# Tiles that DMA fills on 256-byte boundaries, in chunked attention followed by a routed expert layer

## The chip, the core and the metric

The kernel runs on one core of one Trainium2 chip. The metric is the device time of one execution in microseconds (us). Before the change three runs took 704.83, 706.77 and 709.05 us; the median is 706.77 us. A separate execution was recorded by the hardware profiler. Engines are named as in the profile: PE is TensorE, with PEld for its weight loads; DVE is VectorE; ACT is ScalarE; POOL is GpSimd; SP is SyncE. L12 means line 12 of the kernel before.

## What is computed

Attention inside chunks of 64 tokens, then a layer in which a router gives each token to one of eight experts. Everything is fp32.

```python
# q, k, v: (B=8, H=8, S=576, Dh=64); chunks of 64 tokens, each on its own
scores = q_c @ k_c.T / sqrt(64);  attn = softmax(scores);  x = attn @ v_c
x = x.transpose(0, 2, 1, 3).reshape(4608, 512)            # N tokens, D
logits = (x / |x|) @ (expert_emb / |expert_emb|).T / tau   # 8 experts
e = argmax(logits);  gate = softmax(logits)[e]
out = gate * (relu(x @ w1[e]) @ w2[e])                     # w1: 512x1024, w2: 1024x512
```

## The kernel before

**Attention.** The 4608 tokens are taken as 36 tiles of 128 tokens (two chunks each). For each tile the kernel loads q and k (`load_qk`, L560: 128 partitions, eight pieces of 64 floats, that is 256 bytes, per partition), turns them with TensorE (`turn_qk`, L583), multiplies q by k (`scores`, L599), subtracts the maximum and takes the exponential, turns the result (`turn_a`, L625), multiplies it by v (`values`, L639) and divides, which leaves 128 token rows in a slot of `xr`. The stages of successive tiles are interleaved in a loop that is written out by hand, and every engine works through its own list in program order. The loads of q and k go four tiles ahead, into four buffers each; from the fifth tile on they are issued by GpSimd, while SyncE issues v (`load_v`, L572), one batch of 576 tokens at a time into one of two tiles `v_sb`. Before the loads of the fifth tile GpSimd also writes all constants (`constants`, L497 to L533), among them zeros in the tails of `xr` and in `blank`.

**The token store.** A router (`turn_x`, `logits`, `pick`, `place`) finds the expert of each token and its place in a store in device memory, `spots`, one region per expert. Every token is one record: 512 floats of x and a tail of 16 floats with its eight logits, its token number and the sum of its squares. `xr` has eight such records per partition, one for each of the last eight tiles. One put per tile (`put`, L779), an indirect DMA that GpSimd issues, scatters 128 records into the store. `xr`'s slot is written again eight tiles later; L656 is the first write into it. At the start SyncE clears the first rows of two experts' regions from `blank` (`clear_first`, L540 and L544), and four last puts write `blank` into the places left empty.

**The expert layer.** Blocks of 128 rows (two groups of 64, one for each half of the experts) are loaded from the store by SyncE (`load_rows`, L145, in pieces of 128 floats, and L151 for the tail), three blocks ahead in `xin`. TensorE multiplies them by w1 (L245 for the first blocks; L334, in a form with seven products of half size that works on sums of weight blocks) and by w2 (`result`, L405); GpSimd scatters the rows to the output (L420). Weights for the first blocks come with `load_first` (L120). Later ones come with `load_when` (L169), which SyncE issues only where a block's expert differs from that in the buffer, into `w2_sb` or `next_w1`.

**Where tiles lie.** Tiles are given addresses inside a partition one after another in the order in which they are allocated, pool after pool: `keep` (weights, block numbers, `xin`, `spot`), `blk`, then for the attention `qk`, `work` and `one` (v, `xr`, constants). When these three are closed, pool `late` takes their place for w2's second buffers, `next_w1`, `sums` and the work tiles of the products. The first user of such a tile waits for the last users of what lay there before.

Of the kernel before, what the change touches and what calls it, by code (L numbers as in the profile page):

```python
# [9 lines left out]
FP32 = mybir.dt.float32  # L10
# [8 lines left out]
P = 128  # L19
# [6 lines left out]
def kernel(  # L26
# [11 lines left out]
    nc = tc.nc  # L38
    B, H, S, Dh = q.shape
    E, D = moe_expert_emb.shape  # L40
    F = moe_w1.shape[2]
    N = B * S
    NPAIR = H // 2
# [3 lines left out]
    NCB = S // CH  # L47
    G = P // 2
# [11 lines left out]
    XBUF = 3  # L60
# [9 lines left out]

    MW = 16
    W = D + MW
    TOK, SQ = E, E + 1
    R = N + G * NE
    SPARE = E * R
    spots = nc.dram_tensor("spots", (SPARE + G, W), FP32, kind="Internal").ap()

    keep = ctx.enter_context(tc.tile_pool(name="keep", bufs=1))  # L80
    ctx.enter_context(tc.manual_schedule())

    w1_sb = [keep.tile([P, KD, F], FP32, name=f"w1_{s}") for s in range(2)]
    w2_sb = [[keep.tile([P, KF, D], FP32, name=f"w2_{s}0")] for s in range(2)]

    w1_rows = moe_w1.rearrange("e (p c) f -> p e (c f)", c=KD)
    w2_rows = moe_w2.rearrange("e (p c) d -> p e (c d)", c=KF)
# [15 lines left out]
    n_steps = keep.tile([1, 1], I32, name="n_steps")  # L105
    n_odd = keep.tile([1, 1], I32, name="n_odd")
    second = keep.tile([P, 1], FP32, name="second")
    xin_sb = [keep.tile([P, D], FP32, name=f"xin{i}") for i in range(XBUF)]
    SPOTS = 8
    spot = keep.tile([P, SPOTS, MW], FP32, name="spot")  # L110
    bp = ctx.enter_context(tc.tile_pool(name="blk", bufs=2))

    def whole(w):
# [12 lines left out]
    xin, mo = {}, {}  # L126
# [10 lines left out]
    def load_rows(j, rows):  # L137

        xin[j] = xin_sb[j % XBUF]
        ins = []  # L140
        for s in range(2):
            for b in range(G // Q if s < len(rows) else 0):
                c = s * (G // Q) + b
                ins.append(
                    nc.sync.dma_start(  # L145
                        out=xin[j][:, c * P : c * P + P],
                        in_=rows[s][Q * b : Q * b + Q, 0:D].rearrange("i (r d) -> r i d", d=P),
                    )
                )
            ins.append(  # L150
                nc.sync.dma_start(out=spot[G * s : G * s + G, j % SPOTS], in_=rows[s % len(rows)][:, D:W])  # L151
            )
        return ins

    def load_x(j):
        rows = []
        for s in range(2 if j != LEAST else 1):
            row = number(src_row[of_step(s, j)], SPARE, ENG.SP)
            rows.append(spots[ds(row, G), :])
        load_rows(j, rows)  # L160

    def first_rows(s, j, n):
        r0 = (0, E - 1)[s] * R + G * j
        return spots[r0 : r0 + G * n, :]
# [44 lines left out]
    def gate_parts(j):  # L209
        lg = spot[:, j % SPOTS, 0:E]  # L210
        rn = bp.tile([P, 1], FP32, tag="rn", name="rn", bufs=4)
        lmax = bp.tile([P, 1], FP32, tag="lmax", name="lmax", bufs=4)
        sh = bp.tile([P, E], FP32, tag="sh", name="sh", bufs=4)
        last = "_last" if j == LEAST - 1 else ""
        gate = bp.tile([P, 1], FP32, tag="gate" + last, name="gate", bufs=5)
        nc.scalar.activation(rn, spot[:, j % SPOTS, SQ : SQ + 1], AF.Sqrt)  # L216
        yield
        nc.vector.tensor_reduce(lmax, lg, axis=AX.X, op=ALU.max)
        nc.vector.tensor_scalar(rn, rn, 1e-6, None, ALU.add)  # L219
        nc.vector.reciprocal(rn, rn)  # L220
        nc.vector.tensor_scalar(sh, lg, lmax, rn, ALU.subtract, ALU.mult)
        yield
        nc.scalar.activation(sh, sh, AF.Exp, accum_out=gate)  # L223
        yield
        nc.vector.tensor_scalar(gate, gate, 1e-9, None, ALU.add)
        nc.vector.reciprocal(gate, gate)
        gate_of[j] = gate
# [169 lines left out]
    def result(j, ps_y):  # L397
# [15 lines left out]
        nc.scalar.activation(y[:, 0:w], ps[:, 0:w], AF.Copy, scale=gate_of.pop(j))  # L413
        to, at, bound = out, spot[:, j % SPOTS, TOK : TOK + 1].bitcast(I32), N - 1
        if one_group:
# [18 lines left out]
    RB = 4  # L434
    sizes = [RB] * (NT // RB)
    batch_of = [(b, i) for b, n in enumerate(sizes) for i in range(n)]
    VW = 72
    with (
        tc.tile_pool(name="qk", bufs=4) as qk_p,
        tc.tile_pool(name="work", bufs=2) as wk,  # L440
# [4 lines left out]
        tc.tile_pool(name="ps_l", bufs=1, space=PSUM) as ps_l,  # L445
    ):

        ident = one.tile([P, P], FP32, name="ident")
        make_identity(nc, ident)
        rt_ps = ps_l.tile([P, 4, RB, E], FP32, name="rt_ps")  # L450
# [4 lines left out]
        enT = one.tile([P, KD, E], FP32, name="enT")  # L455


        v_sb = [one.tile([P, NPAIR, NCB, VW], FP32, name=f"v{i}") for i in range(2)]
        onesb = one.tile([P, P], BF16, name="onesb")
        sltb = one.tile([P, P], BF16, name="sltb")  # L460

        NX = 2 * RB
        xr = one.tile([P, NX, W], FP32, name="xr")
        blank = one.tile([P, W], FP32, name="blank")
        io_i = one.tile([P, NST], I32, name="io_i")
        io = one.tile([P, NST], FP32, name="io")
        back = one.tile([P, NST], FP32, name="back")
# [28 lines left out]
        def constants():  # L496
# [3 lines left out]
            nc.gpsimd.memset(onesb, 1.0)  # L500
            nc.gpsimd.memset(xr[:, :, D:W], 0.0)
            nc.gpsimd.memset(blank, 0.0)
# [34 lines left out]
        def clear_first():  # L537

            for s in range(2):
                nc.sync.dma_start(  # L540
                    out=first_rows(s, 0, NE).rearrange("(j p) w -> p j w", p=G),
                    in_=blank[0:G].unsqueeze(1).to_broadcast([G, NE, W]),
                )
# [86 lines left out]
        def values(t):  # L630
# [3 lines left out]
            for i in range(NPAIR):  # L634
# [13 lines left out]
            nc.vector.reciprocal(rs, rs)  # L648
            x = xr[:, t % NX, 0:D]
            nc.vector.tensor_tensor(  # L650
# [5 lines left out]
            nc.gpsimd.iota(  # L656
                xr[:, t % NX, D + TOK : D + TOK + 1].bitcast(I32),
                pattern=[[0, 1]],
# [5 lines left out]
        def turn_x(t):  # L664
            d = st[t]
            ps = ps_t.tile([P, KD, P], FP32, tag="tr", name="tr")
            for c in range(KD):
# [5 lines left out]
            nc.scalar.activation(  # L673
                junk, d["x"], AF.Square, accum_out=xr[:, t % NX, D + SQ : D + SQ + 1]
            )
# [14 lines left out]
        def copy_logits(b):  # L690
            n, t = sizes[b], sum(sizes[:b])
            copied[b] = xr[:, t % NX : t % NX + n, D : D + E]
            nc.vector.tensor_copy(copied[b], rt_ps[:, b % 2, 0:n])
# [17 lines left out]
        def place(b):  # L711
# [33 lines left out]
            if t + n < NT:  # L745
                with nc.allow_low_precision("whole numbers up to 36 + 128"):
                    if n == 1:
                        nc.vector.tensor_tensor(before, before, eqb[:, t], ALU.add)
                    else:
# [5 lines left out]
                        )  # L755
            to_put.extend((dest[:, i : i + 1], xr[:, (t + i) % NX]) for i in range(n))

# [15 lines left out]
        def load_early(j):  # L773
            early_ins.extend(load_rows(j, [first_rows(s, j, 1) for s in range(2)]))
# [289 lines left out]
        behind()  # L1064

    late_p = ctx.enter_context(tc.tile_pool(name="late", bufs=1, reuse_waits="tile"))
    for s in range(2):
        w2_sb[s].append(late_p.tile([P, KF, D], FP32, name=f"w2_{s}1"))

# [7 lines left out]
    with (  # L1077
# [18 lines left out]
        for j in range(LEAST - 1):  # L1096
            n = j + 2
# [104 lines left out]
```

## Time and profile before

| | us |
|---|---|
| median of three runs (lowest, highest) | 706.77 (704.83, 709.05) |
| the profiled execution's own time | 710.12 |
| its span, from first to last instruction | 708.3 |
| PE busy in the span | 651.9 (92%) |
| DVE busy | 426.4 (60%) |
| ACT busy | 441.9 (62%) |
| POOL busy | 160.3 (23%) |
| mean granted TensorE clock | 0.961 |
| moved by DMA | 111.65 MB in 92,670 packets, 50,316 of them under 512 bytes |

The profile is of one execution, and sums over it are compared with its own time. A group's line gives the source line, the engine, the operation, the tiles written and read, then busy time and idle time ahead with what ended it. The granted clock is the share of full speed that TensorE was allowed. The DMA share is the busy time of the core's 16 DMA engines, averaged; [...]it can pass 1. Beside the page, the trace records every DMA packet: its queue, its start, how long it took and its size.

### The profile page before, as it was taken

What the parts mean: (1) busy time and instruction counts of PE and PEld (TensorE: products, weight loads), DVE (VectorE), ACT (ScalarE), POOL (GpSimd) and SP (SyncE); (2) the same over time, 40 slices, a digit from 0 to 9 for tenths busy, and PEclk for the clock granted to TensorE, in tenths of its full rate; (3) what the DMA queues carried; (4) which work ended last, traced back from release to release, by engine and by line L of the source; (5) the groups of instructions that cost most, each with busy time, mean ns of one, the idle gap of its engine ahead of it and who ended that gap; (6) DMA issues with size and microseconds to landing.
All of it is one profiled execution on the core that took longest, in us unless ns stands there. A gap on an engine that the chain in (4) does not pass through costs nothing. (4 is left out here: it accounts for less than half of the span.)

```text
span 708.3 us, 24825 instructions
## 1 busy us (share of the span) xinstructions
PE 651.9 (92%) x9735; PEld 384.7 (54%) x9735; DVE 426.4 (60%) x1139; ACT 441.9 (62%) x767; POOL 160.3 (23%) x241
## 2 busy tenths in 40 slices
PE   3699898998999897999999999999999999999991
PEld 2489797998754343666643444444444443444430
DVE  2478786586649853554766565776665567565520
ACT  3266565464522574767777877877777767877640
POOL 7747676473322110101000101000000100100101
PEclk9799999698999998999999999999999999999996
DMA  9989999798971771111477511486741114411110
GB/s 192 212 187 226 234 240 234 179 230 210 341 276 55 288 281 38 45 46 33 139 298 273 174 43 37 153 315 241 270 171 47 49 40 158 166 41 32 48 33 29
DMA packets 92670, 111.65 MB, mean 158 GB/s; under 512 B 50316, under 2 KB 70540, under 8 KB 92536
## 3 DMA queue, kind: packets, MB, share of 16 engines
q1 hardware_dynamic: 80552, 72.21, 34.4%
q0 software_dynamic: 11952, 37.67, 19.4%
q8 instruction: 81, 1.33, 0.8%
q14 instruction: 53, 0.43, 0.2%
q10 hardware_dynamic: 32, 0.02, 0.0%
HBM read 334.71 MB, written 21.60 MB: 503 GB/s over the span
## 5 line engine op out<-in xcount | busy, mean ns | idle before, releaser
L405 PE MATMUL y_ps<-w,hT 128*32 128x512 f32 (+1 forms) x2368 | 274.5, 590 | 4.1 <-DMA w<-in_moe_w_dram 4.1
L353 ACT ACTIVATE h<-C 64x256 f32<-64x256 f32 x264 | 178.4, 676 | 95.9 <-DVE C L366 70.8
L405 PEld LDWEIGHTS y_ps<-w,hT 128*32 128x32 f32 x2368 | 95.6, 111 | 153.2 <-issue 122.8
L420 POOL DMA_INDIRECT out_dram<-y,spot x36 | 35.0, 971 | 438.8 <-ACT C L369 208.7
L366 DVE TENSOR_TENSOR C<-C,h 128x256 f32<-128x256 f32 x231 | 96.1, 417 | 46.6 <-DVEq L291 39.7
L334 PE MATMUL h<-w,S 128*32 128x256 f32 x1056 | 98.0, 379 | 2.0 <-DVE w L283 2.0
L334 PE MATMUL h<-sums,xbT 128*32 128x256 f32 x1056 | 97.4, 379 | 0.0
L334 PE MATMUL h<-w,xbT 128*32 128x256 f32 x1056 | 79.3, 380 | 6.6 <-ACTq L291 5.4
L360 DVE STREAM_TRANSPOSE hT<-h 128x512 f32<-128x512 f32 x66 | 46.8, 708 | 45.3 <-ACT h L353 45.2
L334 PEld LDWEIGHTS h<-w,xbT 128*32 128x32 f32 x1056 | 41.3, 110 | 42.5 <-ACTq L291 13.7
L334 PEld LDWEIGHTS h<-w,S 128*32 128x32 f32 x1056 | 49.6, 110 | 23.8 <-DVE w L283 1.5
L670 ACT COPY xT<-tr 128x512 f32<-128x512 f32 x36 | 21.1, 587 | 65.4 <-PE tr L668 65.4
L334 PEld LDWEIGHTS h<-sums,xbT 128*32 128x32 f32 x1056 | 49.6, 110 | 20.6
L219 DVE TENSOR_SCALAR rn<-rn 128x1 f32<-128x1 f32 x37 | 5.7, 153 | 73.3 <-ACT rn L216 73.3
L334 PE MATMUL h<-sums,S 128*32 128x256 f32 x528 | 48.6, 379 | 0.0
L195 DVE STREAM_TRANSPOSE xbT<-xin 128x256 f32<-128x256 f32 x73 | 46.8, 679 | 0.5 <-DVE hT L360 0.5
L779 POOL DMA_INDIRECT spots<-xr,dest x36 | 37.1, 1031 | 43.3 <-ACT aT L627 12.3
L216 ACT ACT_TABLE_LOAD x34 | 43.6, 1283 | 0.9 <-issue 0.3
L223 ACT ACT_TABLE_LOAD x34 | 43.6, 1283 | 0.6
L413 ACT ACTIVATE y<-y_ps,gate 128x512 f32<-128x512 f32 (+1 forms) x37 | 25.3, 683 | 29.8 <-issue 16.3
L588 DVE COPY qxT<-tr 128x512 f32<-128x512 f32 x36 | 24.8, 689 | 24.8 <-PE tr L583 23.5
L607 DVE TENSOR_REDUCE mx<-sc 128x8 f32<-128x512 f32 x36 | 24.9, 692 | 22.6 <-PE sc L599 22.5
(195 smaller groups left out, 879.3 us busy)
## 6 DMA issues: line engine op xcount, KB each, us to landing
w<-in_moe_w_dram SPq DMA_DIRECT2D x74, 2048.0 KB
next_w<-in_moe_w_dram SPq DMA_DIRECT2D x67, 2048.0 KB
xin<-spots SPq DMA_DIRECT2D x158, 64.0 KB
qx<-in_q_dram POOLq DMA_DIRECT2D x32, 256.0 KB, 7.5
v<-in_v_dram SPq DMA_DIRECT2D x56, 144.0 KB
kx<-in_k_dram POOLq DMA_DIRECT2D x28, 256.0 KB, 7.6
spot<-spots SPq DMA_DIRECT2D x80, 4.0 KB
spots<-blank SPq DMA_DIRECT2D x2, 528.0 KB
```

The source lines that it names most:

```text
L195: nc.vector.transpose(xT[:, :, cols].rearrange("p c (b i) -> p b c i", i=Q), t[:, s * (D // 2) : (s + 1) * (D // 2)].rearrange("p (b i c) ...
L216: nc.scalar.activation(rn, spot[:, j % SPOTS, SQ : SQ + 1], AF.Sqrt)
L223: nc.scalar.activation(sh, sh, AF.Exp, accum_out=gate)
L334: nc.tensor.matmul(ps[t0 : t0 + Q], lhsT=a[:, c, s], rhs=w[:, r], start=c == 0, stop=c == KD // 2 - 1,)
L353: nc.scalar.activation(h[b][G * v : G * v + G, s].rearrange("p (k i) -> p k i", i=Q), x[G * s : G * s + G].rearrange("p (i k) -> p k i", i=Q),
L360: nc.vector.transpose(hT.rearrange("p k (s b i) -> p b s k i", b=2, i=Q)[:, b], h[b].rearrange("p s (k i) -> p s k i", i=Q),)
L366: nc.vector.tensor_tensor(out, a, b, op)
L405: nc.tensor.matmul(ps[Q * r : Q * r + Q, 0:w], lhsT=d["hT"][:, c, Q * t0 : Q * t0 + Q], rhs=w2_sb[s][buf_of(j)][:, c, d0 : d0 + w], start= ...
L413: nc.scalar.activation(y[:, 0:w], ps[:, 0:w], AF.Copy, scale=gate_of.pop(j))
L420: ins = nc.gpsimd.indirect_dma_start(out=to, out_offset=bass.IndirectOffsetOnAxis(ap=at, axis=0), in_=y[:, 0:w], in_offset=None, bounds_ch ...
L607: nc.vector.tensor_reduce(mx, sc, axis=AX.X, op=ALU.max)
L779: ins = nc.gpsimd.indirect_dma_start(out=spots, out_offset=bass.IndirectOffsetOnAxis(ap=at, axis=0), in_=m, in_offset=None, bounds_check=S ...
```

## The change

Tiles that a DMA fills are allocated together, behind small pad tiles that bring their first byte to a multiple of 256 in the partition. There are four pads, `pad_keep`, `pad_one`, `pad_qk` and `pad_late`; each is filled once by GpSimd. `xin` and `spot` move up to stand behind the weights in pool `keep`; v, `xr` and `blank` move to the front of pool `one`. A row of v, of which 65 floats are used, now takes 128 floats (512 bytes) where it took 72 (288 bytes). A token record takes 576 floats (2304 bytes) where it took 528 (2112 bytes), in `xr`, in `blank` and in the store; the 48 new floats are zeros that nothing reads. The loads of the tail still take 16 floats.

```diff
     MW = 16
-    W = D + MW
+    W = D + 64
+    RW = D + MW
...
+    def pad(pool, n, name):
+
+        if n:
+            nc.gpsimd.memset(pool.tile([P, n], FP32, tag=name, name=name, bufs=1), 0.0)
+
+    pad(keep, 32, "pad_keep")
     w1_sb = [keep.tile([P, KD, F], FP32, name=f"w1_{s}") for s in range(2)]
     w2_sb = [[keep.tile([P, KF, D], FP32, name=f"w2_{s}0")] for s in range(2)]
+    xin_sb = [keep.tile([P, D], FP32, name=f"xin{i}") for i in range(XBUF)]
+    SPOTS = 8
+    spot = keep.tile([P, SPOTS, MW], FP32, name="spot")
...
-                nc.sync.dma_start(out=spot[G * s : G * s + G, j % SPOTS], in_=rows[s % len(rows)][:, D:W])
+                nc.sync.dma_start(out=spot[G * s : G * s + G, j % SPOTS], in_=rows[s % len(rows)][:, D:RW])
...
-    VW = 72
+    VW = 2 * Dh
...
+        pad(one, 40, "pad_one")
+        v_sb = [one.tile([P, NPAIR, NCB, VW], FP32, name=f"v{i}") for i in range(2)]
+        NX = 2 * RB
+        xr = one.tile([P, NX, W], FP32, name="xr")
+        blank = one.tile([P, W], FP32, name="blank")
+        pad(qk_p, 40, "pad_qk")
         ident = one.tile([P, P], FP32, name="ident")
...
-        v_sb = [one.tile([P, NPAIR, NCB, VW], FP32, name=f"v{i}") for i in range(2)]
...
-        NX = 2 * RB
-        xr = one.tile([P, NX, W], FP32, name="xr")
-        blank = one.tile([P, W], FP32, name="blank")
...
     late_p = ctx.enter_context(tc.tile_pool(name="late", bufs=1, reuse_waits="tile"))
+    pad(late_p, 40, "pad_late")
```

More of the change, by code (lines that the diff above doesn't have):

```diff
@@ L107 @@
     second = keep.tile([P, 1], FP32, name="second")
-    xin_sb = [keep.tile([P, D], FP32, name=f"xin{i}") for i in range(XBUF)]
-    SPOTS = 8
-    spot = keep.tile([P, SPOTS, MW], FP32, name="spot")
     bp = ctx.enter_context(tc.tile_pool(name="blk", bufs=2))
```

## The prediction

> **What bounds the kernel now.** I read the table of stages first (busy time of each engine, granted TensorE clock, DMA share, GB/s; the second number on a line is the stretch's length):
>
> ```profile
> core 0: us, PE busy (x) PEld busy (x) DVE busy (x) ACT busy (x) POOL busy (x), PEclk, DMA share, GB/s
> 0.00:35.00 35.00, 16.89 (x232) 13.48 (x236) 10.91 (x23) 10.53 (x17) 27.01 (x70) 0.80 1.08 202
> 35.00:123.70 88.70, 82.60 (x1761) 75.34 (x1754) 66.10 (x160) 53.84 (x120) 56.44 (x78) 1.00 1.07 224
> 123.70:137.40 13.70, 13.29 (x155) 12.13 (x154) 7.31 (x21) 5.79 (x12) 4.88 (x7) 0.50 0.60 160
> ...
> 277.00:700.00 423.00, 410.21 (x5520) 200.22 (x5512) 245.01 (x650) 301.97 (x473) 32.06 (x33) 1.00 0.35 121
> ```
>
> Three stages. In the first 35 us TensorE works half the time, at a clock of 0.80, while the DMA engines are full (1.08): transfers bound this stage. From 35 to 205 us they stay nearly full, but TensorE is busy 82.60 of 88.70 us, so TensorE bounds it. From 277 us on it is busy 97%, and DMA runs at 0.35. Next the chain of waits, TensorE alone: the bracket is the idle time ahead of a line and what ended it.
>
> ```profile
> 3.98 1.09 PE L583 MATMUL tr<-ident,kx 128*128 128x128 f32 x4 [3.98 <-DMA kx<-in_k_dram]
> 7.19 1.12 PE L583 MATMUL tr<-ident,qx 128*128 128x128 f32 x4 [2.13 <-DMA qx<-in_q_dram]
> 17.35 1.08 PE L583 MATMUL tr<-ident,qx 128*128 128x128 f32 x4 [5.15 <-DMA qx<-in_q_dram]
> 28.73 1.09 PE L583 MATMUL tr<-ident,kx 128*128 128x128 f32 x4 [5.20 <-DMA kx<-in_k_dram]
> 31.45 1.09 PE L583 MATMUL tr<-ident,qx 128*128 128x128 f32 x4 [1.63 <-DMA qx<-in_q_dram]
> ...
> 124.11 0.69 PE L599 MATMUL sc<-kxT,qxT 64*64 64x64 f32 x11 [2.33 <-issue]
> ...
> 272.33 9.68 PE L405 MATMUL y_ps<-w,hT 128*32 128x512 f32 x62 [4.14 <-DMA w<-in_moe_w_dram]
> ```
>
> After 31.45 us TensorE waits for no q, k or v of any size: a tile of 128 tokens takes 4.1 to 4.3 us (scores begin at 42.73, 46.82, 50.91, 55.00), and GpSimd, which issues the loads, idles for a free q or k buffer instead. So faster transfers are worth something in the first 31 us, little after. The last line is a late issue, not a slow transfer: SyncE issued this conditional load at 272.13, after issuing row loads from 266.21 on, and no weight packet moved between 262 and 272.
>
> **The change, part by part.** By the addresses in the built programs, the q and k tiles start 224 bytes past a multiple of 256 before and on one after; the weight tiles go from 128 past to 0, xin and spot from 224 to 0, v from 32 and 160 past with rows 288 apart to 0 with rows 512 apart. Every engine has the same instructions in the same order, except for four small fills that GpSimd gains.
>
> *What a 256-byte boundary is worth to a packet.* The record of DMA packets can tell, because v already holds both kinds: with rows of 288 bytes, one in nine begins on a multiple of 256. In v's load near 134.5 us, which has the engines to itself, one engine's run of packets (ns taken / ns since the one before) reads
>
> ```
> 15/- 15/15 18/12 18/14 18/14 18/14 18/14 18/14 18/14 18/12 18/14 18/14 18/12 18/14 18/12 18/13 18/14 18/13 18/14 18/14 ...
> ```
>
> and goes on at 18/14 to the end of its 42 packets, one in nine of them aligned; 15 ns stand near the head of a run, for q/k tiles (never aligned) too. So: 0 ns for an aligned destination. At the source end the rows of the token store, 2112 bytes apart, begin on a boundary in one of four; of the 20,224 packets of 512 bytes that read them, 15,709 took 27 ns and 422 took 25. Again no two groups.
>
> The Trainium skill says otherwise ("DMA: Bandwidth & Descriptors", section "How a descriptor splits into AXI transactions"): a transaction must start at a multiple of 256, so a piece that starts 224 bytes past one is fetched as a whole 256 bytes for its last 32, and then 224: 15 beats of 32 bytes for 8. It describes reads. If engine time followed beats at the writing end, the start's serial legs would shrink to 8/15. These legs are qx 1.50 to 7.19, qx 11.07 to 17.35, and kx with qx from 21.79 to 31.45 (GpSimd's issue to TensorE's start): 5.7 + 6.3 + 9.7 = 21.7 us, so an estimate of 10.1 us by the rule and 0 by the row. I take the row. What it cannot tell is crowded engines: in the first 31.5 us a 4096-byte packet of GpSimd's loads (16 pieces of 256 bytes) took 329 ns in the mean, against 16 x 14.2 = 227 ns at v's undisturbed pace. If alignment won all of that, (329 - 227)/329 = 31% of 21.7 = 6.7 us. Bounds 0 and -6.7; value 0, the only measured case.
>
> *More bytes.* A token record grows from 2112 to 2304 bytes, +192. The 36 puts (L779): 128 x 192 = 24.6 KB each, 0.11 us of the engines at 224 GB/s. They lie beside TensorE-bound work, and GpSimd, with 0.9 + 0.9 us of load issues, 0.15 of L656 and 1.05 of a put, has 1.1 us of every 4.1 us tile free; without that cover 36 x 0.11 = 4.0 us. What is late next, if a put is late, is the reuse of its slot in xr, where GpSimd's L656 already waits 18.8 us in all; behind it in that queue are the next tiles' q and k, which are used four tiles (16.4 us) after their issue and land in 7. So 0. The clearing of the first rows (L540, L544) grows by 0.11 MB, 0.5 us of the engines at 202 GB/s, beside the start's q/k loads: bounds 0 and 0.5, value 0.1, since its packets run from 16.9 to 22.1, and the kx that TensorE waits for at 28.73 is only issued at 21.79.
>
> *GpSimd's queue at the start.* This row prices the fills (start, length):
>
> ```profile
> 13.73 0.20 POOL L501 MEMSET xr<- 128x128 f32 x1
> 13.88 0.54 POOL L502 MEMSET blank<- 128x528 f32 x1
> 14.47 0.10 POOL L503 MEMSET blank<- 128x1 int32 x1
> 14.51 0.10 POOL L504 MEMSET ones<- 128x8 f32 x1
> ...
> 21.79 1.50 POOL L560 DMA_DIRECT2D kx<-in_k_dram  x2 [0.22 <-issue]
> ```
>
> Three fills of 32 or 40 elements now stand ahead of ident and of every q load: small fills follow one another in 0.04 us, so 0.12 us (0.30 if each held the queue for its whole 0.10). The fill of xr grows from 8 x 16 to 8 x 64 elements: (0.54 - 0.20)/400 = 0.85 ns an element, 384 x 0.85 = +0.33; blank gains 48 elements, +0.04. Behind them, in order, wait all the constants and then kx and qx of the fifth tile, issued at 21.79, and TensorE is idle for these at 28.73 with nothing to cover it. So +0.12 + 0.33 + 0.04 = +0.49 us on the path. The fourth fill, pad_late, stands after the last put and ahead of the first output scatter, shares its place with pad_qk alone, and GpSimd is 10% busy there: 0.
>
> *Waits that move with the addresses.* next_w1_1 no longer lies over xr, so its first load loses three waits; C now lies over xr and blank, so its first use at 238.74 (L369) gains waits for the puts. The last of these was issued at 217.7 and landed 2.4 us later, 18 us ahead: 0. Behind that copy ScalarE holds a tile's gates, and TensorE's next products would be late if it were not so. The first sums_1 subtraction (233.17) drops the same finished waits: 0. Conditional weight loads at 4096 bytes took 159 ns from 128 past a boundary, and the output's packets, of which y is aligned before, 159 too (1739 of 2302): 0; the late issue at 272.13 stays.
>
> *Sum.* 0 + 0.1 + 0.49 = +0.6 us. On the profiled execution: span 708.3 + 0.6 = 708.9, with 1.8 us around it (710.12 - 708.3) 710.7. That execution lay 3.35 us above the median of 706.77; the same +0.6 on the median gives 707.4.
>
> **Rivals.** *Alignment pays where the engines are crowded.* For it: DMA share 1.08 and 329 ns where 227 would do. Against: two queues that take turns on each engine explain a longer packet as well. Worth half to all of 6.7 us, 707.4 - 3.4 = 704.0 to 707.4 - 6.7 = 700.7, and emptier engines could also remove a gap at "issue" (the 2.33 us at 124.11, with 13.7 us at half clock behind it: 2.3 + 6.8 = 9.1), which makes 698 or less. I put it at 702.
>
> *The clock falls once more (slower).* Place: any TensorE gap between 35 and 277 us. The stretch 123.70:137.40 ran at 0.50 after a gap of only 2.33 us; others followed 166.85 (a gap of 1.84) and 272.33. The record of the granted clock has half-clock stretches of 6.8 and 13.7 us there, so the price is 3.4 us for each 6.8. The Trainium skill ("TensorE: Matmul & The Clock Gate", section "Part 1: The HAM clock gate (the "warmup" mystery)") has the clock fall after an idle window of about 3.4 us, and the window run free of the kernel. By that rule gaps of 2 us cost nothing and mine would change no clock; by the row a gap of 2 us that falls badly costs 3.4, and a start 0.6 us later moves every gap against the window. Without any new gap: 707.4 + 3.4 = 710.8; it decides from one more such stretch per run. Against: before has the same lottery, and a median averages it.
>
> *The rule holds in full:* 707.4 - 10.1 = 697.3. The 18/14 row speaks against it.
>
> **How the numbers follow.** About 0.5% (3.5 us; the three runs spread from 704.83 to 709.05) is what a measurement of this kernel can tell from no change. No effect but the +0.6: 0.50, with its own range 704 to 710. Crowded engines gain: 0.24, and the full rule 0.03, nearly all below 703.2. Slower clock: 0.23, nearly all above 710.3. Hence faster 0.26, same 0.52, slower 0.22. Cutting a tenth from each side: 699 to 712.
>
> **What would show each step.** Right: v's uncrowded packets still 18 ns at a pace of 14; TensorE's waits near 17.35 and 28.73 within 0.6 us of before, GpSimd's kx issue at about 22.3; a fill of xr at 0.5 us; scores still 4.1 us apart; weight packets at 159 ns; weight-stage TensorE busy 97%. Wrong: packets of q and k clearly below 329 ns in the start and TensorE in its steady pace by 28 us (the first rival); more or longer stretches of half clock (the second); a GpSimd wait at L656 that now reaches TensorE as a wait for kx.

## The result and the profile after

Four runs of the changed kernel took 686.30 to 690.14 us, median 688.75; four runs of the kernel before, beside them, took 704.83 to 709.05, median 707.65. The ratio is 0.9734 with a 95% interval of 0.9691 to 0.9777: about 19 us faster, where the prediction had 707.4 and a range of 699 to 712. The profiled execution of the changed kernel took 686.30 us, with a span of 684.5; that of the kernel before took 710.12, with a span of 708.3. So the two traces differ by 23.8 us, more than the medians do. Executions now and then run some per cent slower as a whole; the ratios leave them out, and the one profile of such an execution (of the kernel with longer records alone, span 718.0) isn't read.

Line numbers have moved by 10 in the attention stage (L583 is now L593, L716 is L726) and by 8 in the expert layer (L405 is L413). The stages of the changed kernel, in the columns shown before:

```profile
core 0: us, PE busy (x) PEld busy (x) DVE busy (x) ACT busy (x) POOL busy (x), PEclk, DMA share, GB/s
0.00:35.00 35.00, 22.02 (x301) 18.02 (x302) 12.94 (x27) 13.00 (x22) 29.04 (x75) 0.85 0.95 241
35.00:123.70 88.70, 88.65 (x1916) 81.42 (x1917) 73.36 (x181) 57.82 (x130) 60.88 (x86) 1.00 0.87 242
123.70:137.40 13.70, 13.66 (x281) 12.43 (x280) 11.63 (x33) 8.99 (x21) 9.99 (x14) 1.00 0.98 281
...
277.00:684.00 407.00, 386.93 (x5204) 175.69 (x5194) 233.95 (x624) 288.42 (x451) 30.01 (x31) 0.99 0.35 123
```

In the first 35 us TensorE is busy 22.02 us instead of 16.89. From 35 to 123.7 us the DMA engines are busy 0.87 instead of 1.07 while they move more per second (242 instead of 224 GB/s), and TensorE has no idle time left: 88.65 of 88.70 us, where it had 82.60. The 13.7 us after that, at half clock before, run at full clock. In the expert stage the DMA share is 0.35 as before and TensorE is busy 95% (97% before). (A share above 1 needs no second queue: v's undisturbed packets take 18 ns each and follow one another every 14, so that they overlap on their own queue. The share compares kernels; it doesn't say by itself when the engines are full.)

TensorE's own lines with an idle time ahead, from 13 us to the first late load of weights:

```profile
13.35 1.09 PE L593 MATMUL tr<-ident,qx 128*128 128x128 f32 x4 [1.10 <-DMA qx<-in_q_dram]
25.68 1.09 PE L593 MATMUL tr<-ident,kx 128*128 128x128 f32 x4 [5.56 <-DMA kx<-in_k_dram]
27.60 1.09 PE L593 MATMUL tr<-ident,qx 128*128 128x128 f32 x4 [0.84 <-DMA qx<-in_q_dram]
148.92 0.34 PE L649 MATMUL pv<-v,aT 64*64 64x65 f32 x5 [0.92 <-issue]
167.37 0.18 PE L726 MATMUL rt_ps<-eqb_all,sltb 128*128 128x32 bf16 x1 [1.12 <-DVE eqb_all L717]
185.30 0.18 PE L726 MATMUL rt_ps<-eqb_all,sltb 128*128 128x32 bf16 x1 [0.76 <-DVE eqb_all L717]
...
217.91 0.62 PE L342 MATMUL h<-w,S 128*32 128x256 f32 x4 [0.96 <-DVE w L291]
219.58 1.10 PE L342 MATMUL h<-w,S 128*32 128x256 f32 x10 [1.04 <-DVE w L291]
...
251.14 7.81 PE L413 MATMUL y_ps<-w,hT 128*32 128x512 f32 x62 [2.13 <-DVE C L374]
```

And those of the kernel before, of which the prediction showed only the first part and one gap:

```profile
41.24 0.33 PE L583 MATMUL tr<-ident,kx 128*128 128x128 f32 x1 [0.81 <-issue]
77.03 0.33 PE L599 MATMUL sc<-kxT,qxT 64*64 64x64 f32 x3 [0.31 <-issue]
84.49 0.21 PE L639 MATMUL pv<-v,aT 64*64 64x65 f32 x1 [1.83 <-issue]
115.33 0.63 PE L583 MATMUL tr<-ident,kx 128*128 128x128 f32 x4 [1.17 <-DVE xr L650]
124.11 0.69 PE L599 MATMUL sc<-kxT,qxT 64*64 64x64 f32 x11 [2.33 <-issue]
166.85 0.34 PE L639 MATMUL pv<-v,aT 64*64 64x65 f32 x5 [1.84 <-issue]
188.30 0.18 PE L716 MATMUL rt_ps<-eqb_all,sltb 128*128 128x32 bf16 x1 [1.12 <-DVE eqb_all L707]
206.14 0.18 PE L716 MATMUL rt_ps<-eqb_all,sltb 128*128 128x32 bf16 x1 [0.77 <-DVE eqb_all L707]
```

The last line of that list, the last rank product (the product of `eqb_all` and `sltb` with which the router's last batch ends), is a mark that both kernels have: 206.14 and 185.30 us. So 20.84 of the 23.8 us are won ahead of it. They split into four terms. A stretch at half clock in which TensorE is never idle costs half its length (from 123.70 to 137.40 us the kernel before did 155 products at half clock, the changed one 281 at full), so half the time at half clock is counted, as an estimate.

| up to the last rank product, us | before | after | difference |
|---|---|---|---|
| end of the last start wait (for qx) | 31.45 | 27.60 | -3.85 |
| gaps at "issue" after it | 7.12 | 0.92 | -6.20 |
| other gaps after it | 3.06 | 1.88 | -1.18 |
| half of the time at half clock after it (27.4 and 8.1 us) | 13.71 | 4.05 | -9.66 |
| the rest: TensorE at work | 150.80 | 150.85 | +0.05 |

That the rest is equal to 0.05 us says that the four terms hold the whole difference of these two executions (over all the runs below the rest varies by 3 us). Behind the mark 502.2 us have become 499.2: the wait for the late issue at 272.33, 4.14 us with 6.8 us at half clock around its end, is one of 2.13 at 251.14 with none (SyncE issued the load at 250.93); 3.4 us at half clock lie at 220.0, behind the gaps of 0.96 and 1.04.

The packets themselves, from the record of each one, in ns. A "packed" packet is one of GpSimd's loads of q and k that carries 16 pieces of 256 bytes; "lone" is the median of those packed packets with no packet of v beside them; the other values are means where nothing else is said:

| packets | before | after |
|---|---|---|
| q and k by GpSimd, 16 pieces of 256 bytes, first 31.5 us | 329.5 | 212.4 |
| the same, lone | 268 | 194 |
| v, one piece of 256 bytes, first 31.5 us | 25.2 | 18.8 |
| v with no packed packet near | 18.8 | 18.2 |
| weights, 4096 bytes in one piece (median) | 159 | 159 |
| instructions, 16 KB, up to 205 us | 1199 | 1074 |

The page's sums per queue say the same, before and then after (packets, MB, share of 16 engines; q0 is GpSimd's queue):

```profile
q1 hardware_dynamic: 80552, 72.21, 34.4%
q0 software_dynamic: 11952, 37.67, 19.4%
```

```profile
q1 hardware_dynamic: 80552, 72.32, 33.2%
q0 software_dynamic: 11952, 38.56, 17.0%
```

As many packets and 0.9 MB more on q0, in a share of a span that is itself shorter.

### The profile page after: what moved, and what is told of

It is laid out like the page before. It is cut to its first block, busy times and chain, and to the rows that moved or that the text cites. A ratio compares the mean times of both kernels' runs of the same rounds, so it can differ in the third digit from the quotient of the medians.

```text
span 684.5 us, 24832 instructions
## 1 busy us (share of the span) xinstructions
PE 643.0 (94%) x9735; PEld 363.4 (53%) x9735; DVE 423.5 (62%) x1139; ACT 441.5 (65%) x767; POOL 160.5 (23%) x245
## 5 line engine op out<-in xcount | busy, mean ns | idle before, releaser
L413 PE MATMUL y_ps<-w,hT 128*32 128x512 f32 (+1 forms) x2368 | 274.4, 587 | 2.3 <-DVE C L374 2.1
L413 PEld LDWEIGHTS y_ps<-w,hT 128*32 128x32 f32 x2368 | 87.5, 110 | 159.6 <-issue 145.6
L342 PE MATMUL h<-w,S 128*32 128x256 f32 x1056 | 101.1, 380 | 2.0 <-DVE w L291 2.0
L342 PE MATMUL h<-sums,xbT 128*32 128x256 f32 x1056 | 101.1, 383 | 0.0
L342 PE MATMUL h<-w,xbT 128*32 128x256 f32 x1056 | 80.7, 380 | 6.4 <-ACTq L299 5.2
L342 PEld LDWEIGHTS h<-w,S 128*32 128x32 f32 x1056 | 48.0, 110 | 25.2 <-DVE w L291 1.5
L342 PEld LDWEIGHTS h<-sums,xbT 128*32 128x32 f32 x1056 | 48.4, 111 | 22.5 <-issue 0.8
L203 DVE STREAM_TRANSPOSE xbT<-xin 128x256 f32<-128x256 f32 x73 | 44.2, 644 | 0.5 <-DVE hT L368 0.5
L421 ACT ACTIVATE y<-y_ps,gate 128x512 f32<-128x512 f32 (+1 forms) x37 | 25.2, 682 | 29.0 <-issue 12.8
L690 PEld LDWEIGHTS rt_ps<-enT,xT 128*128 128x128 f32 x288 | 35.0, 192 | 1.1 <-issue 0.8
L570 POOL DMA_DIRECT2D kx<-in_k_dram x36 | 31.6, 881 | 16.0 <-PE tr L593 15.2
```

The costliest lines, as they stand in the source:

```text
L203: nc.vector.transpose(xT[:, :, cols].rearrange("p c (b i) -> p b c i", i=Q), t[:, s * (D // 2) : (s + 1) * (D // 2)].rearrange("p (b i c) ...
L342: nc.tensor.matmul(ps[t0 : t0 + Q], lhsT=a[:, c, s], rhs=w[:, r], start=c == 0, stop=c == KD // 2 - 1,)
L413: nc.tensor.matmul(ps[Q * r : Q * r + Q, 0:w], lhsT=d["hT"][:, c, Q * t0 : Q * t0 + Q], rhs=w2_sb[s][buf_of(j)][:, c, d0 : d0 + w], start= ...
L570: eng.dma_start(out=x[done : done + n], in_=src[b, :, s : s + n, :].rearrange("h p d -> p h d"),)
L690: nc.tensor.matmul(rt_ps[:, batch_of[t][0] % 2, batch_of[t][1]], lhsT=d["xT"][:, c], rhs=enT[:, c], start=(c == 0), stop=(c == KD - 1),)
```

## The experiments

### Which part of the change pays

Four kernels each do one part alone, or undo one. q and k alone on boundaries:

```diff
 # kernel before
+        pad(qk_p, 8, "pad_qk")
         ident = one.tile([P, P], FP32, name="ident")
```

> The kernel before with the q and k tiles alone moved from 224 past a multiple of 256 to 0 (a pad of 8 floats ahead of them); rows of v stay 288 bytes apart, records 2112. Theory Q (a piece of 256 bytes that straddles a boundary costs GpSimd's packed q/k packets extra, and the crowd then slows v): nearly all of the gain, 690 to 695 us, GpSimd's packets in the first 31.5 us down from 329 to about 215 ns in the mean, v beside them from 25 to about 19 ns. Theory V (the rows of v): 704 to 708 us and unchanged q/k packets. Theory R (records of 2304 bytes): 707 us.

v alone, rows of 512 bytes that begin on boundaries:

```diff
 # kernel before
-    VW = 72
+    VW = 2 * Dh
...
+        pad(one, 56, "pad_one")
         v_sb = [one.tile([P, NPAIR, NCB, VW], FP32, name=f"v{i}") for i in range(2)]
```

> The kernel before with v alone changed: rows 512 bytes apart, first row on a boundary; q and k stay 224 past one, records 2112 bytes. Theory Q: 703 to 708 us, q/k packets still above 270 ns. Theory V: 690 to 695 us, and both v and q/k packets short, because the crossing writes of v held the engines. Theory R: 707 us.

Token records of 2304 bytes alone:

```diff
 # kernel before
-    W = D + MW
+    W = D + 64
+    RW = D + MW
...
+        pad(one, 56, "pad_one")
         xr = one.tile([P, NX, W], FP32, name="xr")
```

> The kernel before with the token records alone changed: 2304 bytes apart in xr, in blank and in the store, xr and blank on a boundary. Theories Q and V: 707 to 709 us (36 longer puts and a fill that is 0.33 us longer). Theory R: 690 to 700 us, with shorter puts and fewer waits of GpSimd at the first write into xr.

The changed kernel with q and k back at 224 bytes past a boundary:

```diff
 # kernel after
-        pad(one, 40, "pad_one")
+        pad(one, 48, "pad_one")
...
-        pad(qk_p, 40, "pad_qk")
+        pad(qk_p, 96, "pad_qk")
```

> The changed kernel with q and k alone put back to 224 past a boundary; v, records and weights stay on boundaries. Theory Q: the gain goes, 703 to 708 us, q/k packets near 300 ns again. Theory V: 689 to 692 us. Half of each: 697 to 700 us.

Measured, as ratios to the kernel before beside them on the same chip (the ratios are those on record, not quotients of the medians): q and k alone 0.9780 (0.9729 to 0.9832), 695.55 us; v alone 0.9829 (0.9768 to 0.9890), 698.30; records alone 0.9993 (0.9938 to 1.0049); all but q and k 0.9791 (0.9731 to 0.9850), 698.16. So records are worth nothing that shows (within 4 us), q with k some 15 us, v some 12, both together 19: less than the sum. That v pays at all is the surprise, for its undisturbed packets take 18 ns with or without a boundary. With v alone moved, v's packets in the start take 22.5 ns and the lone packed ones still 268; with q and k alone moved, 21.2 and 195. The mean of all packed packets in the start, 329.5 before and 212.4 after, is 265.5 with q and k alone moved, where about 215 was expected, and 268.1 with v alone moved, which moves none of them: each kind of packet is shorter when the other is.

### Are q, k and v the whole of it, and which boundary is it

The next four ran beside one another on one chip (kernel before 714.92 us there). First q, k and v without records, weights or slot tokens, and the changed kernel again as the mark:

```diff
 # kernel before
-    VW = 72
+    VW = 2 * Dh
...
+        pad(qk_p, 8, "pad_qk")
         ident = one.tile([P, P], FP32, name="ident")
...
+        pad(one, 48, "pad_one")
         v_sb = [one.tile([P, NPAIR, NCB, VW], FP32, name=f"v{i}") for i in range(2)]
```

> The kernel before with the tiles of q and k and the rows of v on boundaries, and nothing else: token records 2112 bytes apart, weights and slot tokens where they were. Theory (q/k and v are the whole of the change's gain; records, weights and slot tokens are worth nothing): the time of the changed kernel, ratio to the kernel before 0.973, 687 to 692 us; mean packed q/k packet of the first 31.5 us 212 ns, v packet there 18.8 ns. Rival (records or weights on boundaries are part of the gain, hidden in the run with records alone by its noise): ratio 0.98 or more, 694 us or more.

> The changed kernel, unchanged, as the mark for the other three on the same chip: 686 to 692 us, ratio to the kernel before 0.973.

0.9706 (0.9670 to 0.9742) against 0.9718 (0.9681 to 0.9755), 693.62 and 693.56 us. All of the gain that shows, to the 0.4% of these intervals, is in the addresses of q, k and v; both are above the expected microseconds because this chip was slower for the kernel before too.

Then q and k at 128 bytes past a boundary, v's rows 512 apart but 224 past one, and (in the next group) q and k at 192:

```diff
 # kernel after, q and k at 128
-        pad(one, 40, "pad_one")
+        pad(one, 8, "pad_one")
...
-        pad(qk_p, 40, "pad_qk")
+        pad(qk_p, 72, "pad_qk")
```

> The changed kernel with the tiles of q and k moved to 128 bytes past a boundary of 256; everything else stays on boundaries. Theory (a 256-byte piece that straddles a multiple of 256 costs more, wherever it straddles): as with q/k 224 past a boundary, 696 to 700 us, lone packed packet 270 ns. Rival (a finer granule of 64 or 128 bytes counts, and only the remainder of 32 in the kernel before hurt): as the changed kernel, 687 to 692 us, lone packed packet 194 ns.

```diff
 # kernel after, v's rows at 224
-        pad(one, 40, "pad_one")
+        pad(one, 96, "pad_one")
         v_sb = [one.tile([P, NPAIR, NCB, VW], FP32, name=f"v{i}") for i in range(2)]
+        pad(one, 8, "pad_two")
```

> The changed kernel with v's rows still 512 bytes apart, but every row 224 bytes past a boundary: pitch kept, alignment gone. Theory (alignment of v's rows counts): about the run with q/k alone moved, 693 to 697 us, v packets of the first 31.5 us 21 ns. Rival (the pitch of 512 instead of 288 bytes is what helps v): as the changed kernel, 687 to 692 us, v packets 18.8 ns.

```diff
 # kernel after, q and k at 192
-        pad(one, 40, "pad_one")
+        pad(one, 56, "pad_one")
...
-        pad(qk_p, 40, "pad_qk")
+        pad(qk_p, 88, "pad_qk")
```

> The changed kernel with q's and k's tiles 192 bytes past a boundary of 256 (a multiple of 64; 224, where they were, is a multiple of 32 alone). At 128 a lone packed packet took 230 ns, at 224 it took 274, on the boundary 194. If being off a multiple of 64 is what adds the second step: 230 ns here. If the uneven cut of a piece (64 and 192 bytes instead of 128 and 128) adds it: 270 ns.

q and k at 128: 0.9791 (0.9753 to 0.9830), 698.55 us, so it loses as much as 224 did; at 192: 0.9829 (0.9760 to 0.9897), two runs. v at 224 with its new pitch: 0.9779 (0.9735 to 0.9823), 699.12 us, as with q and k alone moved (0.9780). It is the boundary of 256 that counts and not the pitch. A lone packed packet takes 194 ns on the boundary, 230 at 128 and 232 at 192, 268 to 274 at 224. These medians are loose: where v has to be away for 1 us on either side they are 254 at 128, 232 at 192 and 267 to 278 at 224, and 233 at 224 in the kernel before with few loads of v (below), while on the boundary they stay at 188 to 194. So a packed packet off the boundary is longer at every offset that was run, but no order among the offsets is shown. At 128 the expectation had 270 by the theory and 194 by the rival, and neither came. At 192 the account by multiples of 64 bytes (230) came and that by the uneven cut (270) didn't; but since 224 once has 233 too, what sets the size stays open.

### Is it the packets' own time or the crowd

Two kernels leave out six of the eight loads of v (the first two batches' values are used again), which empties the engines without moving an address:

```diff
 # kernel before, and the same in the kernel after
                 if b not in v_t and b < B:
-                    load_v(b)
+                    if b < 2:
+                        load_v(b)
+                    v_t[b] = v_sb[b % 2]
```

> The kernel before, with v loaded for the first two batches alone and used again for the other six: six of eight v loads (12 MB of 16 MB would be two of eight; 1.18 MB each, in pieces of 256 bytes) are left out, so the values and with them the tokens' experts are others, and the stage of the experts may take another time. Read at the last rank product of the attention stage, 206.1 us in the kernel before and 185.3 in the changed one; q and k stay off their boundary. Theory (the packets' cost matters because the DMA engines are full, and what costs is the gaps and the half clock after them): with the crowd gone the gaps at issue and the half clock behind the start go although q and k are still off, and it comes at 187 to 192 us (206.1 less 7.4 of gaps and up to 9.7 of half clock, the start kept). Rival (packets off a boundary cost TensorE time in themselves, by the late landing of q and k): 200 us or later.

> The changed kernel with the same six v loads left out (values and tokens' experts are others). Theory: little is left to gain, since the changed kernel has hardly a gap behind its start: last rank product at 183 to 187 us, 3 to 5 us before that of the kernel before with the same loads left out (the start). Rival (the crowd still costs the changed kernel): 180 us or earlier.

(The first expectation has its megabytes wrong: six loads of 1.18 MB, 7.1 of 9.4 MB, are left out.) The kernel before with fewer loads, a line of the stages and the mark:

```profile
35.00:123.70 88.70, 88.49 (x1906) 81.31 (x1905) 71.27 (x173) 57.17 (x127) 59.54 (x83) 0.99 0.72 188
```

```profile
187.81 0.18 PE L716 MATMUL rt_ps<-eqb_all,sltb 128*128 128x32 bf16 x1 [0.76 <-DVE eqb_all L707]
```

The changed kernel with fewer loads, the mark:

```profile
183.18 0.18 PE L726 MATMUL rt_ps<-eqb_all,sltb 128*128 128x32 bf16 x1 [0.76 <-DVE eqb_all L717]
```

With q and k still 224 bytes off, TensorE has 88.49 of 88.70 us at work, 0.16 us of gaps at issue in all, and the mark comes at 187.81 (187 to 192 expected, 200 by the rival). The changed kernel gains only 2.1 us from the same loads left out. So without the crowd the addresses are worth 4.6 us, of which the start is 3.8 (31.97 to 28.21); with it, 20.8. (The whole times, 710.82 and 704.39 us, can't be compared with the others: other values send tokens to other experts, and the part behind the mark takes 519.9 us instead of 502.2 in the kernel before.)

The other way round: the changed kernel with 26 loads of 256 KB more, into two spare tiles that nobody reads.

```diff
 # kernel after
+        more = [one.tile([P, H, Dh], FP32, name=f"more{i}") for i in range(2)]
...
+            if 0 <= t < 26:
+                b1, s1 = t % B, P * (t % 4)
+                nc.sync.dma_start(
+                    out=more[t % 2], in_=k[b1, :, s1 : s1 + P, :].rearrange("h p d -> p h d")
+                )
```

> The changed kernel with 26 more loads of 256 KB, in pieces of 256 bytes onto boundaries, one a step in the attention stage on SyncE's queue, into a spare tile that nobody reads: 26,624 packets of 18.7 ns are 31 us of all 16 engines, about what the change took off them (4,480 packed packets by 73 ns and 38,912 of v by 6.2 ns: 35 us). Theory (DMA engines that are full make the gaps and the half clock, aligned or not): the gain is given back in good part, last rank product at 195 us or later, 700 us or more, gaps at issue again. Rival (alignment acts on the packets' landing, not through the load of the engines): 693 us or less.

```profile
35.00:123.70 88.70, 85.35 (x1811) 77.62 (x1811) 69.57 (x172) 55.68 (x124) 58.60 (x81) 0.98 1.06 288
123.70:137.40 13.70, 13.20 (x184) 11.98 (x185) 6.13 (x12) 4.77 (x10) 5.77 (x9) 0.64 0.87 218
```

```profile
120.22 1.09 PE L650 MATMUL pv<-v,aT 64*64 64x65 f32 x8 [1.01 <-DMA v<-in_v_dram]
121.84 0.96 PE L650 MATMUL pv<-v,aT 64*64 64x65 f32 x8 [0.53 <-DMA v<-in_v_dram]
124.18 0.97 PE L650 MATMUL pv<-v,aT 64*64 64x65 f32 x6 [1.38 <-DMA v<-in_v_dram]
```

0.9873 (0.9815 to 0.9931), 696.45 us, mark at 192.46: between the two accounts, and for another reason than either. The DMA share is back at 1.06, but there is no gap at issue at all. TensorE waits for v, which stands behind the added loads on SyncE's queue, and 13.7 us at half clock follow. The account that a full DMA share by itself makes the gaps fell here, for this queue. Two further kernels ask what does: the same loads 224 bytes off, and the same loads on boundaries but issued by ScalarE.

```diff
 # the kernel with more loads
+        pad(one, 56, "pad_more")
         more = [one.tile([P, H, Dh], FP32, name=f"more{i}") for i in range(2)]
+        pad(one, 8, "pad_ident")
```

> The changed kernel with the same 26 loads more, but their spare tile 224 bytes past a boundary, so that each of the 26,624 pieces straddles one; same bytes, same queue, same steps as the run with them on boundaries, which had no gap at issue, fetches of instructions of 1,026 ns and the last rank product at 192.5 us. Theory now (pieces that straddle a boundary, in a crowd, hold up the fetch of instructions; bytes alone don't): gaps at issue come back, 2 us or more up to the last rank product, fetches there 1,100 ns or longer, the product at 196 us or later, 699 us or more. Rival (the gaps at issue come by other chance, not by straddling): as with the loads on boundaries, less than 1 us of gaps at issue, product at 190 to 195 us.

```diff
 # the kernel with more loads
-                nc.sync.dma_start(
+                nc.scalar.dma_start(
                     out=more[t % 2], in_=k[b1, :, s1 : s1 + P, :].rearrange("h p d -> p h d")
```

> The changed kernel with the same 26 loads more on boundaries, issued by ScalarE instead of SyncE, so that v is not queued behind them. Theory now (bytes on boundaries are borne without loss; the waits for v and the half clock after them came from SyncE's queue): no waits for v, gaps at issue under 1 us, last rank product at 185 to 189 us, ratio to the kernel before 0.97 to 0.98. Rival (the crowd itself costs, straddling or not): 192 us or later, ratio 0.985 or more.

Off the boundary: 0.9852 (0.9772 to 0.9932), 699.40 us, mark at 195.40, 1.79 us of gaps at issue, and 1107 ns in the mean for the packets that bring instructions. That is on the theory's side, but each value is at its edge or short of it, and the time can't be told from that with the loads on boundaries (0.9873). From ScalarE:

```profile
74.60 0.66 PE L679 MATMUL tr<-ident,xr 128*128 128x128 f32 x4 [0.47 <-issue]
81.77 0.33 PE L636 MATMUL tr<-ident,a 128*128 128x128 f32 x1 [1.31 <-issue]
119.74 0.48 PE L610 MATMUL sc<-kxT,qxT 64*64 64x64 f32 x4 [1.94 <-issue]
```

No wait for v, as expected, but 3.72 us of gaps at issue with every added piece on a boundary, 13.7 us at half clock behind the last, and the mark at 195.01. So straddling (lying across a boundary) isn't needed: in this execution a crowd of aligned pieces makes these gaps too, coming through another queue. In the whole time the ratio is 0.9753 (0.9649 to 0.9858), 694.79 us, and its four runs spread from 688.31 to 698.23, the profiled one (698.18) near the slow end: the time alone doesn't decide, the trace does.

### All runs beside one another

Up to the mark, of each run's one profiled execution, in us; the gaps at issue up to 137.4 us are given apart, because later ones also stand beside the first weight loads. The records kernel is left out.

| run | DMA share 35 to 123.7 | start ends | gaps at issue (up to 137.4) | other gaps | half of half clock | mark | ratio of times |
|---|---|---|---|---|---|---|---|
| before | 1.07 | 31.45 | 7.12 (5.28) | 3.06 | 13.71 | 206.14 | 1 |
| changed | 0.87 | 27.60 | 0.92 (0) | 1.88 | 4.05 | 185.30 | 0.9734 |
| changed, again | 0.86 | 28.28 | 3.07 (0) | 4.09 | 3.79 | 191.73 | 0.9718 |
| q, k, v only | 0.86 | 27.47 | 2.33 (0) | 2.26 | 9.11 | 195.20 | 0.9706 |
| q, k only | 0.91 | 29.63 | 2.54 (0.38) | 3.65 | 3.40 | 191.66 | 0.9780 |
| v only | 1.03 | 29.06 | 3.60 (0.78) | 3.59 | 5.77 | 194.45 | 0.9829 |
| all but q, k | 1.03 | 30.79 | 3.18 (1.30) | 5.66 | 7.20 | 198.24 | 0.9791 |
| q, k at 128 | 0.99 | 30.03 | 2.74 (0.78) | 3.45 | 3.67 | 192.81 | 0.9791 |
| q, k at 192 | 1.01 | 30.24 | 3.10 (1.79) | 2.57 | 4.67 | 192.68 | 0.9829 |
| v at 224 | 0.94 | 30.36 | 4.88 (1.38) | 5.71 | 6.17 | 199.09 | 0.9779 |
| before, less v | 0.72 | 31.97 | 0.16 (0.16) | 2.21 | 2.79 | 187.81 | |
| changed, less v | 0.60 | 28.21 | 0 (0) | 2.08 | 2.09 | 183.18 | |
| more, SyncE | 1.06 | 27.40 | 0 (0) | 5.30 | 8.74 | 192.46 | 0.9873 |
| more, off boundary | 1.09 | 27.97 | 1.79 (1.79) | 5.99 | 9.30 | 195.40 | 0.9852 |
| more, ScalarE | 1.06 | 29.64 | 3.72 (3.72) | 1.93 | 9.02 | 195.01 | 0.9753 |

What is left of the mark when the four terms are taken off is 150 to 154 us in every row, so the runs' differences are in these four terms to within some 3 us. Up to 137.4 us gaps at issue come with a DMA share of 0.91 or more, and 0.16 us at most below 0.9; the one run that doesn't fit is that with more loads on SyncE's queue. A single profiled execution is a coarse measure: the changed kernel again has 2.15 us more of gaps at issue than at first, and the profiled execution of q, k, v only was the slowest of its four (696.66).

What the engine waits for in these gaps the profile's lines don't say, but the trace's records do. Instructions come in packets of 16 KB on a queue of their own (q8), one every 7 us or so in this stage, and TensorE starts some 250 instructions (weight loads and products counted together) for each. Up to 137.4 us there are 20 gaps at issue of 0.3 us or more, in nine runs. Every one of them stands at the same few places of TensorE's list: behind 705, 1985, 2241, 2497, 4033 or 4289 of its instructions, whatever the kernel. These numbers differ by multiples of 256. And every one ends 1.3 to 1.7 us after such a packet has landed. So TensorE has run out of instructions at the end of a block of 256, and the next block comes late.

Late means that its packet starts late, not that it is long: in these 20 cases it took 0.97 to 1.43 us, but it began 1.9 to 2.5 us ahead of the gap in the sixteen short ones (under 0.9 us) and only 0.35 to 1.2 us ahead of it in the four long ones (1.3 to 2.3 us). The Trainium skill ("DMA: Bandwidth & Descriptors", section "Queues, rings and completion order") has each DMA engine serve its queues in turn, one whole packet from each. A packed packet of 330 instead of 212 ns, or a third queue in the turn, would then lengthen the wait ahead of such a packet, and more packets on a queue that is already busy would not: that fits all three kernels with added loads and the odd one in the table, but no run here shows the turn itself, and why the packets start late stays open.

## Why the prediction was wrong, point by point

**The step that failed** is the value of a boundary to a packet: "So: 0 ns for an aligned destination", and "I take the row". The row was right as far as it went, since v's undisturbed packets still take 18 ns and weight packets 159. But it was a row of single pieces, and the packets whose cost was in question were packed ones of 16. Those could have been read in the same trace: where no packet of v is near, they took 268 ns in the median, 16.8 per piece, above v's pace of 14. On a boundary they take 194, 12.1 per piece. The working explained 329 ns by two queues that take turns; but of the 117 ns by which the mean in the start fell (329.5 to 212.4), the boundaries of q and k alone bring 64, and those of v alone 61.

**The rule that spoke against the row** (the Trainium skill, "DMA: Bandwidth & Descriptors", section "How a descriptor splits into AXI transactions"). Counted its way, a piece takes 15 beats at 224 bytes past a boundary and 8 on it. It describes reads, and these are writes. Its direction held for packed packets, its size didn't: 15/8 of 194 would be 364 ns, an estimate by the rule, where 233 to 278 came.

**"Faster transfers are worth something in the first 31 us, little after"** was the second failure. It looked for waits on q, k and v, rightly found none, and put everything else at nothing. But 7.12 us of gaps at issue, 3.06 of other gaps and 27.4 us at half clock lay between 31 and 206 us, which only their sum shows: 23.9 us of cost, of which 17 went in this pair of executions, and 13 with the second profile of the changed kernel. The prediction named one of these gaps, at 124.11. Its "nearly full" from 35 to 205 us also passed over its own line from 123.70 to 137.40, where the share is 0.60 while TensorE runs at half clock.

**The first rival was right in its mechanism and too small in its size.** It had -3.4 to -6.7 in the start, which gave -3.85, and a single gap with its half clock, 9.1 us, as a possibility "which makes 698 or less". The gaps and the half clock gave 13 to 17 us by the traces. The prediction's own sign of it came: packed packets clearly below 329 ns (212), and TensorE in its pace by 28 us (27.60).

**The smaller terms.** Larger records cost nothing that shows (0.9993 alone, give or take 0.6%; a put's packet takes 191.7 ns at 4608 bytes, 195.6 before at 4224). The fills of xr and blank took the forecast 0.53 and 0.58 us, to 0.01; the pads follow one another in 0.06 to 0.07 us, not 0.04:

```profile
0.81 0.13 POOL L90 MEMSET pad_one<- 128x40 f32 x1
0.87 0.13 POOL L90 MEMSET pad_qk<- 128x40 f32 x1
...
11.94 0.52 POOL L511 MEMSET xr<- 128x512 f32 x1
12.41 0.58 POOL L512 MEMSET blank<- 128x576 f32 x1
...
20.70 1.50 POOL L570 DMA_DIRECT2D kx<-in_k_dram  x2 [0.59 <-PE tr L635]
```

The +0.49 us on the path can't be seen: kx of the fifth tile is issued at 20.70, where 22.3 was forecast and it was 21.79 before, because GpSimd's work ahead of it is done earlier too (the pair of qx loads before it begins at 9.29 instead of 11.07). It even waits 0.59 us for a free buffer, so the fills were covered. The three pads at the very start delay the first qx load by 0.09 us (1.59 instead of 1.50), where 0.12 was forecast. GpSimd's wait for puts (L666, L656 before) fell from 18.8 to 13.0 us.

**The clock.** The slower rival had the price right (3.4 us for each 6.8), and the sign of the draw wrong: fewer gaps drew fewer stretches. The row was the better guide: 13.7 us at half clock followed a gap of 2.33 us in the kernel before, one of 1.94 in the kernel with ScalarE's loads, and one of 1.01 in that with SyncE's (with 0.53 and 1.38 behind it), all shorter than the idle window of 3.4 us that the Trainium skill gives ("TensorE: Matmul & The Clock Gate", section "Part 1: The HAM clock gate (the "warmup" mystery)"). In the 3.4 us ahead of these three stretches TensorE was busy 0.43, 0.54 and 0.77 of the time.

## What to carry to other kernels

Where packets carry many short pieces, compare the time per piece in a quiet place with that of a single-piece packet, before one is taken for the other. Where the DMA share is near 1, a packet's price isn't its time on the chain of waits: add up every gap at issue and half of the time at half clock, over all of the stage, for these are what a lighter load can give back. Look where in an engine's list its gaps at issue stand: the same instruction numbers in several kernels point at the loading of instructions. And parts of a change that lighten the same crowd need not add up: here one alone brought 15 of 19 us.

## What the runs showed of the hardware

- A packed packet of 16 pieces of 256 bytes, written by GpSimd's queue, took 194 ns in the median on a boundary of 256 and 230 to 278 at 128, 192 and 224 past it. Packets of one piece took the same on and off (18 ns for 256 bytes undisturbed, 159 for 4096).
- In a crowd single pieces cost more too: v's packets in the start took 25.2 ns with everything off, 22.5 with v alone moved, 21.2 with q and k alone, 18.8 with both.
- TensorE's 20 gaps at issue of 0.3 us or more up to 137.4 us stand at ends of blocks of 256 of its instructions, 1.3 to 1.7 us behind the landing of a 16 KB packet of instructions; the longest, 2.33 us, had a packet that took 1.09 us but began 0.35 us ahead of the gap.
- Added traffic of 6.8 MB cost TensorE no gap at issue on SyncE's queue and 3.72 us of them on ScalarE's, at the same DMA share of 1.06. Why is open; whether the turn of queues explains it wasn't tried.
- In three kernels 13.7 us at half clock began within a gap of TensorE of 1.0 to 2.3 us, after 3.4 us in which it was busy 0.43 to 0.77 of the time.
